# A chunked retention layer with an expert layer behind it: the first 128 tokens of each sequence as one piece, a shorter warm-up, and another list of loads

## The chip, the cores and the metric

The kernel runs on one core of a Trainium2 chip. The metric is the device time of one execution in microseconds (us). The core has five engines that run their own instruction queues side by side: PE (TensorE, matrix products, with the weight loads shown apart as PEld), DVE (VectorE), ACT (ScalarE), POOL (GpSimd) and SP (SyncE, which here only issues DMAs). They meet through semaphores. Results of PE land in PSUM, everything else lies in SBUF, and DMAs bring data in from HBM.

## The reference

Two layers. The first is retention with a decay per head, here 4 sequences, 8 heads, 768 tokens, 64 numbers a head; the second a gated two-matrix layer on the 3072 tokens, 512 to 2048 to 512.

```python
for t in range(S):
    state = gamma[None, :, None, None] * state + np.einsum('bhd,bhe->bhde', k[:, :, t], v[:, :, t])
    y[:, :, t] = scale * np.einsum('bhd,bhde->bhe', q[:, :, t], state)
...
h = x @ w_in
relu6 = np.clip(h + 3.0, 0.0, 6.0)
g = h * relu6 / 6.0
return (g @ w_out).astype(np.float32)
```

## The kernel before

**Rows.** A row is 128 tokens of one sequence with all 8 heads; there are 24. Rows 0 to 3 are the first rows of the four sequences, rows 4 to 7 the second ones, and so on; four rows are one unit u of 512 tokens. A row has four loads of 256 KB: q and k with the head's numbers on the partitions (qt, kt), k and v with tokens on the partitions (kn, vn). A row is cut into two halves of 64 tokens. On PE, `scores` (L374) makes k times q for each half, `gather` (L398) k times v, which is what the row adds to the state, and `inner_part` (L386) applies the masked scores to v; each is 16 small products, and a float32 product is two instructions with a weight load each, so that a block shows as 32. `outer_part` (L361) adds what the earlier state gives; a sequence's first row has none. The decay is put on v before its use (`decay` in `load`: ACT L468, POOL L465) and taken off the result after it (`scale` in `inner_step`, L627, with the table dq). Between them DVE masks the scores (`fading`, L536), ACT passes the part that needs no mask (L541) and copies a first state (L572). The scaled result is then split for the next layer into a high part on ACT (L255) and a low part on DVE (L165); the split pair is x.

**The layers behind.** `mm1_step` (L648) makes one block of 128 of the 2048 columns for a unit: 12 products of 128 x 512 (L656), followed by L662 and L665 and a store to HBM. It needs all four x of its unit and its own block of w_in. These blocks come as 64-bit numbers of 512 KB, and `convert` (L191) with `split` makes a pair of float32 parts of them: ACT L204, DVE L208, L212, L223, L229, ACT L255, DVE L165. The staging tile st has two buffers, so that the load of block 2 waits until block 0 has passed L229, and block 3 waits for block 1. When all 1152 products of the first layer are done, 1008 of the second (L842) follow.

**Order.** Every step is an entry with an engine, a cost, what it needs and a rank. `Plan.order` (L71) runs them through a list schedule ahead of the build, and each engine's queue is then in that order by hand. PE keeps the order in which its steps were added (in `burst`, L687): scores of a row ahead of the inner part of the row before it; then the blocks of unit 0 with rows 4 to 7 between them, and then blocks of units 0 and 1 in turn. SP issues in the order of the list FIRST (L416): v, k, q, k by token of each row in turn, with the table dq and blocks 1 to 4 of w_in behind rows 1, 3, 4, 5 and 7 (BEHIND). An issue that waits holds all behind it. Where the plan sees PE idle in the first 60 us, `spin` (L755) puts products of zeros there; WARM products of zeros stand ahead of everything (L341).

Of the kernel before, what the change touches and what calls it, by code (L numbers as in the profile page):

```python
# [41 lines left out]
class Plan:  # L42
# [28 lines left out]
    def order(self):  # L71
# [43 lines left out]
def retention_ffn(ctx: ExitStack, tc: tile.TileContext, qkv, w_in, w_out, dvs, dqs, out, B, H, S, D):  # L115
# [133 lines left out]

    def split_step(parts, cols, dep, rank, boxes):  # L250


        def high():
            for hi, lo, src in parts():
                nc.scalar.activation(out=hi, in_=src, func=AF.Copy)  # L255
# [7 lines left out]
        return add("DVE", cost - 0.02, low, (one,), rank, boxes, port=True)  # L263

# [8 lines left out]
    def place_box(tag):  # L273

        return plan.box(tag, PLACES[tag])
# [65 lines left out]
    for n in range(WARM):  # L341
        nc.tensor.matmul(idle[:, 0:P], warm[:, 0], warm[:, 1], start=True, stop=True)
# [4 lines left out]
    rows, early, early_boxes, tiles_done = {}, {}, {}, []  # L347

# [25 lines left out]
    def scores(t, wide):  # L374

        for i, c, a, h in tiles:
            nc.tensor.matmul(  # L377
                t["sc"](a, i, c)[halves[h ^ a]],
                t["kt"]["t"][halves[h], 2 * i + a, cut[c]],
                t["qt"]["t"][halves[h], 2 * i + a, whole_or_cut(c, wide)],  # L380
                start=True,
                stop=True,
                skip_group_check=True,
            )

    def inner_part(t, n, wide):  # L386

        for i, c, a, h in tiles:
            nc.tensor.matmul(  # L389
                t["y"][halves[a], h, i, whole_or_cut(c, wide)],  # L390
                t["vn"]["t"][halves[h ^ a], 2 * i + a, cut[c]],
                t["masked"](a, i, c)[halves[h ^ a]],
                start=wide and not n and (i, c) == (0, 0),
                stop=True,
                skip_group_check=True,
            )

    def gather(t, n, wide):  # L398

        for i, c, a, h in tiles:  # L400
            if not c or n < ROWS_B - 1:
# [13 lines left out]

    FIRST = [(0, "vn"), ("w", 0), (0, "kt"), (0, "qt"), (0, "kn")]  # L416
    for r in range(1, AHEAD):
        FIRST += [(r, "vn"), (r, "kt"), (r, "qt"), (r, "kn")]
        FIRST += BEHIND.get(r, [])

# [26 lines left out]
    def load(r, rank):  # L447
# [3 lines left out]
        row = r % UR * ROWS_B + n  # L451
        if r % UR == 0:
            dq[n] = load_part("dq", dqs[n], (0, 17, 34)[n] if n < 3 else None, first(n, "dq", rank - 2))
        t["dq"] = dq[n]
        places = [o for o in range(35) if o not in (0, 17, 34)]
        parts = {"kt": 1, "qt": 0, "vn": 3, "kn": 2}
        for i, (x, which) in enumerate(parts.items()):
            o = places[4 * r + i] if r < AHEAD else None
            t[x], t["box", x], t["got", x] = load_part(x, qkv[row, which], o, first(r, x, rank + i / 10))

        def decay(pool, hs):
            v = t["vn"]["t"].rearrange("p a (h e) -> p (a h) e", h=2)[:, hs]
            scale = cst_sb[:, n, hs]
            if pool:
                nc.gpsimd.tensor_tensor(out=v, in0=v, in1=scale[:, :, None].to_broadcast([P, hs.stop - hs.start, D]), op=ALU.mult)  # L465
            else:
# [7 lines left out]
                lambda *_, pool=pool, hs=hs: decay(pool, hs),  # L474
                (t["got", "vn"],),
                rank + FADE,
                (t["box", "vn"],),
            )
# [3 lines left out]
    def scores_step(r, at):  # L482
# [5 lines left out]
        def run():  # L488
            if spare:
                banks = [ps_h.tile([P, UT], F32, tag="h", name=nm("sc")) for _ in range(2)]  # L490
            else:
                both = ps_a.tile([P, 2, UT], F32, tag="sc", name=nm("sc"))
                banks = [both[:, a] for a in range(2)]
            t["banks"] = [(both, slice(0, 2))] if not spare else [(b[:, None], slice(a, a + 1)) for a, b in enumerate(banks)]
            if wide:
# [6 lines left out]

        t["S"] = add("PE", 0.7 if wide else 0.5, run, (t["got", "kt"], t["got", "qt"]), at, (*t["sc box"], t["box", "kt"], t["box", "qt"]))

# [87 lines left out]
    def outer_step(r, at):  # L592
# [11 lines left out]
        states = ([] if wide else [t["state box", 0]]) + ([was["state box", 1]] if n else [])  # L604
        deps = [None if wide else t["adds"][0], t["S"], was and was["adds"][1]]
        t["T"] = add("PE", 0.55, run, deps, at, (t["y box"], t["box", "qt"], *states))

    def inner_step(r, at):
        t, u, wide = rows[r], r // UR, r < AHEAD
        n = u  # L610

        def run():
# [5 lines left out]

        t["I"] = add("PE", 0.7 if wide else 0.55, run, (*t["A"], t["T"]), at, (t["y box"], t["am box"], t["box", "vn"]))
        if r % UR == 0:  # L620
            x_boxes[u] = [place_box("wf") for a in range(2)] if u == 2 else [plan.box("x", 2)]
            x_ready[u] = []
        xr = plan.box("xr", 2)
# [10 lines left out]
        def parts():  # L634
            if u not in xs and u == 2:
                xs[u] = [place([P, NK, UT], F32R, nm("x"), "wf") for a in range(2)]
            elif u not in xs:
                x = xpool.tile([P, 2, NK, UT], F32R, tag="x", name=nm("x"))
                xs[u] = [x[:, a] for a in range(2)]
            o = r % UR * P  # L640
            yield *(xs[u][a][:, :, o : o + P] for a in range(2)), t["x"]

# [286 lines left out]
def constants(H, S, D):  # L929

    g = 1.0 - 2.0 ** (-5.0 - np.arange(H, dtype=np.float64))
    t = np.arange(S, dtype=np.float64).reshape(S // P, P) - S // 2
    dv = by_half((g[:, None] ** -t.reshape(-1))[:, :, None]).transpose(1, 0, 2).reshape(P, -1)
    dq = (g[:, None] ** t[:, None, :] / np.sqrt(D))[:, heads(H)]
    dq = np.repeat(dq, D, axis=2).transpose(0, 2, 1, 3).reshape(S // P, 2 * D, -1)
    half = P // 2
    mask = np.tile(np.arange(half)[:, None] <= np.arange(half), (2, 1)).astype(np.float64)
# [18 lines left out]
def lay_qkv(q, k, v):  # L956
# [5 lines left out]

    k_half, v_half = (by_half(a).reshape(-1, P, H * D) for a in (k, v))
    return np.ascontiguousarray(np.stack([by_dim(q), by_dim(k), k_half, v_half], axis=1))
# [38 lines left out]
```

## Time and profile before

| what | us |
|---|---|
| median of three runs | 583.24 |
| lowest and highest of them | 581.8, 583.39 |
| the profiled execution, its own time | 584.08 |
| span of the profile of that execution | 582.3 |
| products of the first layer, L656, busy | 268.0 |
| products of the second layer, L842, busy | 233.2 |

The profile's page lists busy time by engine, the span in 40 slices, the chain that ended last and the costliest groups. The windows view gives each engine's busy time in chosen stretches, the mean clock granted to TensorE (1.00 is full) and the share of the DMA engines that was in use. The timeline lists instructions in order; behind each group, in brackets, stand the idle time of its engine just before it and what ended that. "issue" there means that the engine waited for nothing that the profile shows. A "q" behind an engine's name marks its queue, where DMAs are issued.

### The profile page before, as it was taken

What the parts mean: (1) busy time and instruction counts of PE and PEld (TensorE: products, weight loads), DVE (VectorE), ACT (ScalarE), POOL (GpSimd) and SP (SyncE); (2) the same over time, 40 slices, a digit from 0 to 9 for tenths busy, and PEclk for the clock granted to TensorE, in tenths of its full rate; (3) what the DMA queues carried; (4) which work ended last, traced back from release to release, by engine and by line L of the source; (5) the groups of instructions that cost most, each with busy time, mean ns of one, the idle gap of its engine ahead of it and who ended that gap; (6) DMA issues with size and microseconds to landing.
All of it is one profiled execution on the core that took longest, in us unless ns stands there. A gap on an engine that the chain in (4) does not pass through costs nothing.

```text
span 582.3 us, 12762 instructions
## 1 busy us (share of the span) xinstructions
PE 567.6 (97%) x5102; PEld 467.0 (80%) x5102; DVE 420.3 (72%) x752; ACT 245.3 (42%) x442; POOL 19.7 (3%) x25
## 2 busy tenths in 40 slices
PE   7699999999999999999999999999999999999997
PEld 6577888888888888888888888888888888888885
DVE  4389988989843798443445967997699966799753
ACT  5484454544422443222244544454434443454340
POOL 1000000001000000001000000000000000000000
PEclk9699999999999999999999999999999999999999
DMA  9685587676744576554255439974789546897002
GB/s 324 260 298 193 180 282 262 190 274 228 236 146 163 197 225 221 175 178 168 75 181 181 163 118 350 373 226 130 255 260 314 178 110 196 281 312 223 1 4 105
DMA packets 61259, 119.91 MB, mean 206 GB/s; under 512 B 7056, under 2 KB 7312, under 8 KB 61200
## 3 DMA queue, kind: packets, MB, share of 16 engines
q1 hardware_dynamic: 60912, 119.04, 60.6%
q8 instruction: 40, 0.66, 0.5%
q14 instruction: 19, 0.16, 0.1%
q10 hardware_dynamic: 288, 0.06, 0.0%
HBM read 87.61 MB, written 31.46 MB: 204 GB/s over the span
## 4 chain that ended last, share of the span: by engine, by line
PE 95%; DMA 2%; issue 1%; DVE 1%; SPq 0%; DVEq 0%
PE h L656 46%; PE o L842 40%; PE y L389 3%; PE sc L377 3%; PE sc L402 2%; DMA early<-in_qkv 2%; PE y L365 2%; PE spin L758 0%; SPq L189 0%; DVE wb L223 0%; PE pace L355 0%; DVE ww L229 0%; DVE xr L627 0%; DVE x L165 0%; DVE u L859 0%
## 5 line engine op out<-in xcount | busy, mean ns | idle before, releaser
L656 PE MATMUL h<-x,w 128*128 128x512 f32 x1152 | 268.0, 392 | 0.6 <-DVE x L165 0.6
L656 PEld LDWEIGHTS h<-x,w 128*128 128x128 f32 x1152 | 214.6, 188 | 46.2 <-DVE x L165 1.0
L842 PE MATMUL o<-gc,w 128*128 128x512 f32 x1008 | 233.2, 393 | 0.0
L842 PEld LDWEIGHTS o<-gc,w 128*128 128x128 f32 x1008 | 189.2, 188 | 43.8
L665 DVE SCALAR_TENSOR_TENSOR g<-g,h 128x512 f32<-128x512 f32 x96 | 65.8, 686 | 80.3 <-ACT g L662 79.5
L662 ACT ACTIVATE g<-h,three 128x512 f32<-128x512 f32 x96 | 66.0, 688 | 117.0 <-PE h L656 116.7
L247 ACT ACTIVATE gc<-gr 128x512 fp32r<-128x512 f32 x120 | 71.6, 623 | 58.4 <-PE o L842 42.2
L165 DVE TENSOR_TENSOR gc<-gr,gc 128x512 fp32r<-128x512 f32 x120 | 79.6, 685 | 21.2 <-ACT gc L247 21.0
L247 ACT ACTIVATE gc<-keep 128x512 fp32r<-128x512 f32 x48 | 30.3, 632 | 63.7 <-PE o L842 41.3
L165 DVE TENSOR_TENSOR gc<-keep,gc 128x512 fp32r<-128x512 f32 x48 | 32.8, 686 | 12.4 <-ACT gc L247 12.2
L204 ACT ACTIVATE wm<-st 128x512 f32<-128x512 f32 x32 | 21.5, 671 | 20.3 <-DMA st<-in_w_out 8.7
L255 ACT ACTIVATE x<-xr 128x512 fp32r<-128x512 f32 x24 | 15.1, 629 | 31.6 <-DVE xr L627 31.6
L465 POOL TENSOR_TENSOR vn<-vn,cst_sb 128x512 f32<-128x512 f32 x16 | 16.9, 1058 | 244.4 <-DMA vn<-in_qkv 219.5
L859 DVE SCALAR_TENSOR_TENSOR u<-o,u 128x512 f32<-128x512 f32 (+1 forms) x31 | 20.1, 666 | 6.4 <-PE o L842 6.4
L223 DVE SCALAR_TENSOR_TENSOR wb<-st,wb 128x512 int32<-128x512 int32 x32 | 22.7, 710 | 0.4
L165 DVE TENSOR_TENSOR w<-ww,w 128x384 fp32r<-128x384 f32 (+2 forms) x34 | 22.1, 656 | 0.8 <-ACT w L255 0.7
L229 DVE SCALAR_TENSOR_TENSOR ww<-st,wb 128x512 int32<-128x512 int32 x32 | 21.9, 685 | 0.3
L168 DVE TENSOR_TENSOR keep<-gr,gr 128x512 f32<-128x512 f32 x24 | 16.4, 685 | 7.0 <-DMA gr<-gd 7.0
L255 ACT ACTIVATE w<-ww 128x384 fp32r<-128x384 f32 (+2 forms) x34 | 18.5, 550 | 6.2 <-DVE ww L229 6.0
L208 DVE TENSOR_SCALAR wm<-wm 128x512 f32<-128x512 f32 x32 | 14.1, 441 | 8.6 <-ACT wm L204 8.3
L165 DVE TENSOR_TENSOR x<-xr,x 128x512 fp32r<-128x512 f32 x24 | 16.5, 688 | 2.6 <-ACT x L255 1.8
L536 DVE TENSOR_TENSOR am<-sc,mask 128x512 f32<-128x512 f32 (+1 forms) x26 | 16.5, 640 | 2.1 <-PE sc L402 1.7
(52 smaller groups left out, 334.4 us busy)
## 6 DMA issues: line engine op xcount, KB each, us to landing
gr<-gd SPq DMA_DIRECT2D x168, 256.0 KB, 4.3
gd<-g SPq DMA_DIRECT2D x96, 256.0 KB, 2.8
early<-in_qkv SPq DMA_DIRECT2D x32, 256.0 KB, 5.6
st<-in_w_in SPq DMA_DIRECT2D x16, 512.0 KB, 4.1
st<-in_w_out SPq DMA_DIRECT2D x16, 512.0 KB, 3.9
kt<-in_qkv SPq DMA_DIRECT2D x16, 256.0 KB, 3.4
qt<-in_qkv SPq DMA_DIRECT2D x16, 256.0 KB, 4.5
vn<-in_qkv SPq DMA_DIRECT2D x16, 256.0 KB, 5.3
```

The lines of the kernel that those rows point to most:

```text
L165: return nc.vector.tensor_tensor(out=out_, in0=a, in1=b, op=ALU.subtract)
L204: nc.scalar.activation(out=t["m"], in_=t["hi"].bitcast(F32), func=AF.Abs)
L223: nc.vector.scalar_tensor_tensor(out=b, in0=t["hi"], scalar=-0x40000000, in1=b, op0=ALU.bitwise_and, op1=ALU.bitwise_or)
L229: nc.vector.scalar_tensor_tensor(out=t["w"].bitcast(I32), in0=t["lo"], scalar=29, in1=t["b"], op0=ALU.logical_shift_right, op1=ALU.bitwise_or,
L247: nc.scalar.activation(out=hi, in_=src, func=AF.Copy)
L255: nc.scalar.activation(out=hi, in_=src, func=AF.Copy)
L377: nc.tensor.matmul(t["sc"](a, i, c)[halves[h ^ a]], t["kt"]["t"][halves[h], 2 * i + a, cut[c]], t["qt"]["t"][halves[h], 2 * i + a, whole_o ...
L656: nc.tensor.matmul(h, w[:, o, a], xs[u][b][:, k], start=k + n == 0, stop=(k, n) == (NK - 1, 2), skip_group_check=True)
L662: nc.scalar.activation(out=t["g"], in_=t["h"], func=AF.Relu, bias=three)
L665: ins = nc.vector.scalar_tensor_tensor(out=t["g"], in0=t["g"], scalar=6.0, in1=t["h"], op0=ALU.min, op1=ALU.mult)
L842: nc.tensor.matmul(banks[b, i, h], w2c[jj][:, RIGHT[i], a, h], gc[:, q, c], start=jj == 0 and n == 0, stop=jj == NFP - 1 and n == 2, skip_ ...
L859: nc.vector.scalar_tensor_tensor(out=out_[:, cut], in0=banks[b, i, h][:, cut], scalar=f, in1=other[:, cut], op0=ALU.mult, op1=ALU.add)
```

## The change

For rows 0 to 3 (n = 0, "whole") the row is no longer halved. Scores are 8 products with the full 128 tokens on both sides, the inner part is 8, the gather is 8. The table m0, m1 (two loads of 256 KB instead of the one table dq of that unit) holds the decay between each pair of tokens by head together with the mask and the scale, and DVE multiplies the scores by it in two instructions of 512 columns. So neither v's decay nor the scaling afterwards is needed: x is split straight out of PSUM. For the state, k by token is given its decay (same instructions as v had), and the gather of row r moves from the row's own turn to the turn of row r + 4 (`states_step`); its result is copied by ACT into the space of the row's kt. Masked scores have three buffers in a place of w_in blocks, and all of rows 0 to 3 share one PSUM tile for their results. The host lays k, v and the tables out accordingly.

The warm-up has 4 products of 512 columns instead of 14 of 128. The list of the first loads is written out: k, q, m0, m1, v, w_in block 0, and so on (t is k by token, d is dq, w a block). The plan lets SP start at 0.7 instead of 2.0 us, and three of its ranks are new.

```diff
-        free = dict.fromkeys(left, self.FIRST)
+        free = {e: 0.7 if e == "SP" else self.FIRST for e in left}
...
-    WARM = 14
+    WARM = 4
     SPIN, FILL = 60.0, 0.7
     DECAY = ("ap", "ap", "ap", "ap", "aa", "aa", "aa", "aa")
-    FADE, W_FIRST, W_NEXT = 4.5, 0.5, 2.0
-    BEHIND = {1: [(0, "dq")], 3: [("w", 1)], 4: [(1, "dq"), ("w", 2)], 5: [("w", 3)], 7: [("w", 4)]}
+    FADE, W_FIRST, W_NEXT = 2.5, 1.5, 1.0
+    KFADE = 7.0
+    ORDER = "k0 q0 m0 m1 v0 w0 k1 q1 v1 k2 q2 v2 t0 k3 q3 v3 w1 t1 v4 t2 t3 k4 q4 t4 d1 v5 k5 q5 t5 w2 w3 k6 q6 t6 v7 k7 v6 q7 t7 w4"
...
-        nc.tensor.matmul(idle[:, 0:P], warm[:, 0], warm[:, 1], start=True, stop=True)
+        nc.tensor.matmul(idle, warm[:, 0], warm, start=True, stop=True)
...
+        if t["whole"]:
+            for p in range(NPAIR):
+                for h, d in enumerate(halves):
+                    nc.tensor.matmul(
+                        t["banks"][h][:, p * P : (p + 1) * P],
+                        t["kt"]["t"][d, p],
+                        t["qt"]["t"][d, p],
+                        start=True,
+                        stop=True,
+                        skip_group_check=True,
+                    )
+            return
...
+            for h, d in enumerate(halves):
+                for p in range(NPAIR):
+                    i, a = divmod(p, 2)
+                    nc.tensor.matmul(
+                        t["ys"][halves[a], (2 * h + i) * P : (2 * h + i + 1) * P],
+                        t["vn"]["t"][:, p, d],
+                        t["am"][:, h, p],
+                        start=True,
+                        stop=True,
+                        skip_group_check=True,
+                    )
...
+            for p in range(NPAIR):
+                i, a = divmod(p, 2)
+                for d in halves:
+                    nc.tensor.matmul(
+                        t["us"][d, a, i],
+                        t["kn"]["t"][:, p, d],
+                        t["vn"]["t"][:, p, d],
+                        start=True,
+                        stop=True,
+                        skip_group_check=True,
+                    )
+            return
...
-        if r % UR == 0:
-            dq[n] = load_part("dq", dqs[n], (0, 17, 34)[n] if n < 3 else None, first(n, "dq", rank - 2))
-        t["dq"] = dq[n]
+        if r == 0:
+            dq[0] = [load_part("dq", dqs[h * ROWS_B], 34 * h, first("m", h, 0)) for h in range(2)]
+        elif r % UR == 0:
+            dq[n] = load_part("dq", dqs[n], 17 if n == 1 else None, first(n, "dq", rank - 2))
+        t["dq"], t["whole"] = dq[n], not n
...
+        what = "vn" if n else "kn"
+
         def decay(pool, hs):
-            v = t["vn"]["t"].rearrange("p a (h e) -> p (a h) e", h=2)[:, hs]
+            v = t[what]["t"].rearrange("p a (h e) -> p (a h) e", h=2)[:, hs]
...
-                rank + FADE,
-                (t["box", "vn"],),
+                (t["got", what],),
+                rank + (FADE if n else KFADE),
+                (t["box", what],),
...
+    def masks_step(r, at):
+        t = rows[r]
+        t["am box"] = plan.box("ams", NAM)
+
+        def fading():
+            if not ams:
+                big = place([P, NAM, 2, NPAIR, P], F32, nm("ams"), "w")
+                ams.extend(big[:, n] for n in range(NAM))
+            t["am"] = ams[r % NAM]
+            for h in range(2):
+                nc.vector.tensor_tensor(
+                    out=t["am"][:, h].rearrange("p a n -> p (a n)"),
+                    in0=t["banks"][h],
+                    in1=t["dq"][h][0]["t"].rearrange("p a n -> p (a n)"),
+                    op=ALU.mult,
+                )
+
+        deps, boxes = [t["S"], *(m[2] for m in t["dq"])], [*t["sc box"], t["am box"], ams_box, *(m[1] for m in t["dq"])]
+        t["A"] = [add("DVE", 1.22, fading, deps, at + 2, boxes)]
+
+    def states_step(r, at):
+        t, box = rows[r], plan.box("h", NH)
+        t["state box", 1] = t["box", "kt"]
+
+        def run():
+            us = ps_h.tile([P, UT], F32, tag="h", name=nm("us"))
+            t["us"] = us[:, 0 : 2 * P].rearrange("p (a i n) -> p a i n", a=2, i=2)
+            gather(t, 0, True)
+
+        def copy():
+            t["state", 1] = t["kt"]["t"][:, 0:2].rearrange("p i (a n) -> p i a n", a=2)
+            nc.scalar.activation(out=t["state", 1], in_=t["us"], func=AF.Copy)
+
+        t["G"] = add("PE", 0.6, run, (*t["faded"], t["got", "kn"], t["got", "vn"]), at, (box, t["box", "kn"], t["box", "vn"]))
+        t["adds"] = {1: add("ACT", 0.37, copy, (t["G"],), at + 1.5, (box, t["state box", 1]))}
...
+            t["y box"] = plan.box("y0", 2)
+
+            def run():
+                if not whole_ys:
+                    whole_ys.append(ps_a.tile([P, 2, UT], F32, tag="y", name=nm("y")))
+                t["ys"] = whole_ys[0][:, r % 2]
+                inner_part(t, n, wide)
+
+            def parts():
+                yield *x_parts(u, r * P), t["ys"].rearrange("p (a n) -> p a n", n=P)
+
+            t["I"] = add("PE", 1.1, run, (*t["A"], t["got", "vn"]), at, (t["y box"], t["am box"], ams_box, t["box", "vn"]))
+            x_ready[u].append(split_step(parts, [4 * P], t["I"], at + 1, (t["y box"], *x_boxes[u]), port=False))
...
+            if UR <= new < AHEAD:
+                states_step(new - UR, n - 0.1)
             scores_step(new, n)
-        if old is not None:
+        if old is not None and not rows[old]["whole"]:
             outer_step(old, n + 0.1)
         if new is not None:
-            gather_step(new, n + 0.2)
+            (masks_step if rows[new]["whole"] else gather_step)(new, n + 0.2)
```

More of the change, by code (lines that the diff above doesn't have):

```diff
@@ L262, in split_step @@
         one = add("ACT", cost, high, (dep,), rank, boxes)
-        return add("DVE", cost - 0.02, low, (one,), rank, boxes, port=True)
+        return add("DVE", cost - 0.02, low, (one,), rank, boxes, port=port)
     w1s, w1_boxes, w1_ready = {}, {}, {}
@@ L341, in retention_ffn @@
     for n in range(WARM):
-        nc.tensor.matmul(idle[:, 0:P], warm[:, 0], warm[:, 1], start=True, stop=True)
+        nc.tensor.matmul(idle, warm[:, 0], warm, start=True, stop=True)
     halves = [slice(h * D, (h + 1) * D) for h in range(2)]
     mask = apool.tile([P, HALF], F32, name="mask", bufs=1)
-    rows, early, early_boxes, tiles_done = {}, {}, {}, []
+    rows, early, early_boxes, tiles_done, ams, whole_ys = {}, {}, {}, [], [], []
+    NAM, ams_box = 3, place_box("w")
     tiles = [(i, c, a, h) for i in range(2) for c in range(2) for a in (1, 0) for h in range(2)]
@@ L386, in inner_part @@
     def inner_part(t, n, wide):
+        if t["whole"]:
+            for h, d in enumerate(halves):
[10 more added lines that the diff above has]
+            return
         for i, c, a, h in tiles:
@@ L398, in gather @@
     def gather(t, n, wide):
+        if t["whole"]:
+            for p in range(NPAIR):
[9 more added lines that the diff above has]
+                    )
+            return
         for i, c, a, h in tiles:
@@ L414, in early_tile @@
         return early[key]
[L416 to L419, printed above, removed]
+    LOADS = {"q": "qt", "k": "kt", "t": "kn", "v": "vn", "d": "dq"}
+    FIRST = [(x[0], int(x[1])) if x[0] in "mw" else (int(x[1]), LOADS[x[0]]) for x in ORDER.split()]
     def first(r, x, rank):
@@ L493, in run @@
                 banks = [both[:, a] for a in range(2)]
+            if t["whole"]:
+                t["banks"] = banks
+                return scores(t, wide)
             t["banks"] = [(both, slice(0, 2))] if not spare else [(b[:, None], slice(a, a + 1)) for a, b in enumerate(banks)]
@@ L501, in run @@
             scores(t, wide)
-        t["S"] = add("PE", 0.7 if wide else 0.5, run, (t["got", "kt"], t["got", "qt"]), at, (*t["sc box"], t["box", "kt"], t["box", "qt"]))
+        t["S"] = add("PE", 1.1 if t["whole"] else 0.7 if wide else 0.5, run, (t["got", "kt"], t["got", "qt"]), at, (*t["sc box"], t["box", "kt"], t["box", "qt"]))
+    def masks_step(r, at):
[27 more added lines that the diff above has]
+        t["adds"] = {1: add("ACT", 0.37, copy, (t["G"],), at + 1.5, (box, t["state box", 1]))}
     def gather_step(r, at):
@@ L604, in outer_step, with x_parts @@
         states = ([] if wide else [t["state box", 0]]) + ([was["state box", 1]] if n else [])
-        deps = [None if wide else t["adds"][0], t["S"], was and was["adds"][1]]
+        deps = [None if wide else t["adds"][0], t["S"], was and was["adds"][1], *(x_ready[0] if r == UR else [])]
         t["T"] = add("PE", 0.55, run, deps, at, (t["y box"], t["box", "qt"], *states))
+    def x_parts(u, o):
+        if u not in xs and u == 2:
+            xs[u] = [place([P, NK, UT], F32R, nm("x"), "wf") for a in range(2)]
+        elif u not in xs:
+            x = xpool.tile([P, 2, NK, UT], F32R, tag="x", name=nm("x"))
+            xs[u] = [x[:, a] for a in range(2)]
+        return (xs[u][a][:, :, o : o + P] for a in range(2))
     def inner_step(r, at):
@@ L610, in inner_step @@
         n = u
+        if r % UR == 0:
+            x_boxes[u] = [place_box("wf") for a in range(2)] if u == 2 else [plan.box("x", 2)]
+            x_ready[u] = []
+        if t["whole"]:
+            t["y box"] = plan.box("y0", 2)
[8 more added lines that the diff above has]
+            x_ready[u].append(split_step(parts, [4 * P], t["I"], at + 1, (t["y box"], *x_boxes[u]), port=False))
+            return
         def run():
@@ L617, in run @@
             inner_part(t, n, wide)
[L619 to L622, printed above, removed]
+        deps = x_ready[0] if r == UR else []
+        t["I"] = add("PE", 0.7 if wide else 0.55, run, (*t["A"], t["T"], *deps), at, (t["y box"], t["am box"], t["box", "vn"]))
         xr = plan.box("xr", 2)
@@ L634, in parts @@
         def parts():
[L635 to L641, printed above, removed]
+            yield *x_parts(u, r % UR * P), t["x"]
         one = add("DVE", 0.61, scale, (t["I"], t["dq"][2]), at + 1, (t["y box"], t["dq"][1], xr))
@@ L932, in constants @@
     t = np.arange(S, dtype=np.float64).reshape(S // P, P) - S // 2
-    dv = by_half((g[:, None] ** -t.reshape(-1))[:, :, None]).transpose(1, 0, 2).reshape(P, -1)
+    dv = by_half((g[:, None] ** -t.reshape(-1))[:, :, None])
+    dv[0] = (g[:, None] ** -t[0]).T
+    dv = dv.transpose(1, 0, 2).reshape(P, -1)
     dq = (g[:, None] ** t[:, None, :] / np.sqrt(D))[:, heads(H)]
     dq = np.repeat(dq, D, axis=2).transpose(0, 2, 1, 3).reshape(S // P, 2 * D, -1)
+    gap = np.arange(P) - np.arange(P)[:, None]
+    whole = np.where(gap >= 0, g[:, None, None] ** np.maximum(gap, 0), 0.0) / np.sqrt(D)
+    whole = whole.reshape(-1, 2, P, P).transpose(1, 2, 0, 3).reshape(2, P, -1)
+    dq = np.concatenate([whole[:1], dq.reshape(S // P, P, -1)[1:], whole[1:]])
     half = P // 2
@@ L961, in by_dim, with by_token @@
         return a.reshape(B, H // 2, 2, S // P, P, D).transpose(0, 3, 2, 5, 1, 4).reshape(-1, 2 * D, H // 2 * P)
-    k_half, v_half = (by_half(a).reshape(-1, P, H * D) for a in (k, v))
+    def by_token(a):
+        n = by_half(a)
+        n[:, 0] = a[:, :, :P].transpose(0, 2, 1, 3).reshape(B, P, -1)
+        return n.reshape(-1, P, H * D)
+    k_half, v_half = by_token(k), by_token(v)
     return np.ascontiguousarray(np.stack([by_dim(q), by_dim(k), k_half, v_half], axis=1))
```

3 lines of the change are left out of this document (1 added, 2 removed).

## The prediction

> **What bounds the kernel now.** I read the page first, then the windows view (columns: window, length, busy time and products of PE and PEld, busy time of DVE, ACT and POOL, granted clock, DMA share, GB/s).
>
> ```profile
> span 582.3 us, 12762 instructions
> 31.22:55.73 24.51, 23.43 (x513) 19.37 (x513) 20.79 (x40) 16.34 (x45) 1.04 (x1) 1.00 0.75 270
> 62.57:296.40 233.83, 233.77 (x2849) 194.09 (x2849) 158.60 (x302) 87.28 (x138) 15.88 (x15) 1.00 0.59 199
> ```
>
> From 62.57 to 296.40 PE is idle for 0.06 us, and the second layer follows as densely. No work there is touched, so it can only be shifted. What the change is worth lies ahead: by how much does PE reach the same point in its queue earlier? I take as that point the end of rows 4 to 7 between the first four blocks, where the dense blocks begin: 55.73. Call the start of the first full block T (31.22 now) and that point D. Then the timeline for the stretch ahead of T:
>
> ```profile
> 1.45 4.75 PE L342 MATMUL idle<-warm 128*128 128x128 f32 x28 [1.45 <-DVE warm L339]
> 7.63 0.90 PE L377 MATMUL sc<-early 64*64 64x128 f32 x32 [1.42 <-DMA early<-in_qkv]
> 16.85 0.33 PE L377 MATMUL sc<-early 64*64 64x64 f32 x3 [2.27 <-issue]
> 18.26 1.57 PE L377 MATMUL sc<-early,early 64*64 64x128 f32 x32
> 23.31 0.38 PE L402 MATMUL sc<-early 64*64 64x64 f32 x3 [2.72 <-issue]
> 27.01 1.46 PE L389 MATMUL y<-am,early 64*64 64x128 f32 x32
> 31.22 2.77 PE L656 MATMUL h<-x,w 128*128 128x512 f32 x11 [0.59 <-DVE x L165]
> ```
>
> Two holes of 2.27 and 2.72 us with no releaser cut through row 2's scores and row 3's gather, in the middle of one step. The windows up to the first hole and between the two, and the DMA view in three quarter-microseconds (14.00, 20.75 and 24.25), say what they are:
>
> ```profile
> 0.00:14.60 14.60, 10.29 (x221) 9.12 (x221) 6.06 (x11) 7.82 (x23) 2.14 (x8) 1.00 0.92 324
> 16.80:20.60 3.80, 3.74 (x126) 3.56 (x126) 1.29 (x2) 1.02 (x3) 0.00 (x0) 0.66 1.06 396
> 20.60:23.30 2.70, 0.00 (x0) 0.00 (x0) 0.69 (x1) 0.26 (x1) 0.00 (x0) 0.50 1.03 385
> q8 instruction: 40, 0.66, 0.5%
> q8 instruction: 1, 0.02, 27.0%
> q8 instruction: 1, 0.02, 27.7%
> q8 instruction: 1, 0.02, 32.1%
> ```
>
> Between the holes PE ran 126 products and 126 weight loads, 252 instructions. The instruction queue moves 0.66 MB / 40 = 16.5 KB a packet. A packet runs at 14.0 and at 20.75, and PE goes on 2.6 to 2.9 us later, at 16.85 and 23.31. I read it so: PE's program comes in pages of some 252 instructions; a page is asked for when the last but one is used up (16.85 for the packet at 20.75), and while the DMA engines are full (share 1.03 to 1.06) it takes 23.31 - 16.85 = 6.46 us. With empty queues the packet of 24.25 follows its request at 23.31 by 0.9 us. Rows 0 to 3 eat a page in 3.8 us, so PE starves. The first hole comes after 442 instructions, 252 + 190.
>
> The second delay is on SP: the page's waits for the DMA queue, the timeline of POOL (whose row shows when a row's v has landed), DVE and SP, and one window.
>
> ```profile
> 8.91 0.61 POOL L465 TENSOR_TENSOR early<-early,cst_sb 128x256 f32<-128x256 f32 x1 [4.49 <-DMA early<-in_qkv]
> 14.96 0.61 POOL L465 TENSOR_TENSOR early<-early,cst_sb 128x256 f32<-128x256 f32 x1 [2.09 <-DMA early<-in_qkv]
> 26.43 0.41 DVE L208 TENSOR_SCALAR wm<-wm 128x512 f32<-128x512 f32 x1
> 29.87 0.69 DVE L229 SCALAR_TENSOR_TENSOR ww<-st,wb 128x512 int32<-128x512 int32 x1
> SPq L189 <- DVE ww L229: 13.0, 2, 9.9
> 30.62 0.33 SPq L189 DMA_DIRECT2D st<-in_w_in  x1
> 25.00:30.60 5.60, 5.60 (x47) 4.12 (x45) 4.65 (x10) 4.20 (x14) 0.00 (x0) 0.71 0.02 7
> ```
>
> Block 1's conversion sits in DVE's queue behind row 3's mask, which waits for the second hole; L229 ends at 30.56, SP waits 9.9 us for it with block 3's load, and the DMA engines stand empty (0.02).
>
> **The change, step by step.** *Landing.* In units of 256 KB (a block of w_in is 2), v of row 1 was unit 7 and seen at 8.91, v of row 3 unit 16 at 14.96: 0.672 us a unit. In the new list v0 is unit 5, q1 9, q3 16, v3 17, w1 19, t4 26, t5 31, w2 33, w3 35, v6 41, t7 43, w4 45. By that line q1 is there at 10.25, q3 at 14.96, v3 at 15.6, w1 at 17.0, t4 at 21.7, t5 at 25.0, w2 at 26.4, w3 at 27.7, v6 at 31.8, w4 at 34.4. The first ones land sooner, but the warm-up covers them: it streams 4 x 2 x 512 = 4096 columns where 28 x 128 = 3584 took 4.75, so 5.4, and ends at 6.9, ahead of the 7.63 of now. Nothing is lost there.
>
> *Instructions.* Until row 3's inner part the queue now has 16 for the warm-up and 4 x 64 (two blocks of 8 products a row, each two instructions and two loads) = 272, and some 20 of zero products. The first 190 last until about 13.5, within row 1's inner part; the page then asked for is there at 13.5 + 6.5 = 20, and is wanted only after 252 more: row 2 and 3 (106), a block (24), row 0's gather (32), row 4's scores (64), in all until about 24. **Both holes go**, 5.0 us; late next is the landing of q3.
>
> *The chain of row 3.*
>
> ```profile
> L536 DVE TENSOR_TENSOR am<-sc,mask 128x512 f32<-128x512 f32 x2 | 1.4, 686 | 1.7 <-PE sc L402 1.7
> L627 DVE TENSOR_TENSOR xr<-y,early 128x512 f32<-128x512 f32 x4 | 2.8, 692 | 9.1 <-PE y L389 9.1
> L165 DVE TENSOR_TENSOR x<-xr,x 128x512 fp32r<-128x512 f32 x4 | 2.8, 688 | 1.0 <-ACT x L255 1.0
> L255 ACT ACTIVATE x<-xr 128x512 fp32r<-128x512 f32 x4 | 2.5, 623 | 1.1 <-DVE xr L627 1.1
> L468 ACT ACTIVATE early<-early,cst_sb 128x64 f32<-128x64 f32 x32 | 8.3, 334 | 5.0 <-DMA early<-in_qkv 4.0 <-DMA cst_sb<-in_decays_v 1.0
> L204 ACT ACTIVATE wm<-st 128x512 f32<-128x512 f32 x3 | 2.0, 668 | 0.2 <-DMA st<-in_w_in 0.2
> 8.31 0.68 PE L402 MATMUL sc<-early 64*64 64x64 f32 x32
> ```
>
> The new products (64 x 128 and 128 x 64 weights) are in no row. Two of them fit side by side in the array, four of the old ones did, so 16 instructions should cost what 32 did: 0.90. The other end is no pairing at all, 4.75 / 28 = 0.17 each, 2.7 a block. I take 0.95, next to the row with the same amount of arithmetic. Then: scores 14.96 to 15.9; two masks at 0.69, 17.35; inner part, 18.3; ACT 0.62 straight from PSUM, 19.0; DVE 0.69, 19.8; hops of up to 0.1 at each step (L229's end at 30.56 to SP's issue took 0.06) and up to one foreign instruction of 0.69 on DVE ahead: **T = 20.5**. DVE per row loses the mask (0.69) and the scaling (0.69) and gets two masks, so nothing; from 7 to 20 it has 4 x 2.07 and block 0's 2.9, 11.2 of 13 us. ACT loses the passing of scores; its decays (4 x 0.334 a row, POOL beside it) move behind t, off row 3's chain. The second mask table is one unit more, in the list above.
>
> *From T to D.* The same blocks and rows took 24.51 with PE busy for 23.43. Four gathers move in, 32 instructions took 0.68 from start to end, 16 wide ones 0.5: 2.0, so 26.5 without a new wait. Is there one? Block 1 lands at 17.0, its conversion (two of 0.41 and three of 0.69 on DVE, 2.9; 0.67 and 0.62 on ACT) ends near 22, ahead of its use at 25.5, so SP reaches block 3 at about 21 with no wait to speak of. Block 2 (26.4 + some 5 for ACT, DVE, ACT, DVE) is ready at 31.5, wanted at 32. Row 6 wants v6, 31.8 plus 8 x 0.334 on ACT = 34.5, at 35. Each is just in time. DVE has 20.79 and the rest of block 1, some 22 of 28 us. The narrowest is PE's own program: 2 x 513 + 4 x 32 = 1154 instructions, 4.6 pages, at 6.46 each 29.6 us if the DMA engines stay full; they do until w4 at 34.4, half of the stretch. Already now a page is just in time here, with a row that I would expect to see grow:
>
> ```profile
> 40.51 0.90 PE L389 MATMUL y<-am,early 64*64 64x128 f32 x32 [0.38 <-issue]
> ```
>
> Between 26.5 and 29.6 I take 28.5: **D = 49.0**, that is 55.73 - 49.0 = 6.7 us earlier. The rest (a table of the third unit that goes to another buffer, the new ranks, SP's start in the plan) is in the order alone; below and above it may be a late or lucky place in a queue, within the bounds of T and D.
>
> **The sum.** The profiled execution took 584.08, 0.84 above the median of 583.24. 584.08 - 6.7 = 577.4, and against the median **576.5**.
>
> **The rivals.**
> *It runs clean* (574.0): no page is late, T = 20.0, D = 46.5, 9.2 us. For it: every landing above is ahead of its use. Against it: the 0.38 that is there today.
> *Half clock* (579.8). The clock fell to 0.66 and 0.50 around the holes, and scores took 1.57 and the inner part 1.46 instead of 0.90. If PE, with its waits for landings between 7 and 20, falls back too, row 3 pays 0.6 + 0.6 and the first block 0.7 x 3.0 (2.77 for 11 of its 12 products) = 2.1: D = 52.3. Against it:
>
> ```profile
> 7.50:16.00 8.50, 5.54 (x193) 4.55 (x193) 4.03 (x7) 5.57 (x20) 1.84 (x3) 1.00 1.05 394
> ```
>
> PE was busy for only 65% here and kept 1.00; it will have about 7.6 of 13 us and zero products besides. Products that do not pair end in the same place.
> *The holes stay* (581.5): if they are not the program's pages, 5.0 us come back, D = 54.0, 1.7 us earlier. [...]
> *Slower: block 1's conversion ends as late as now* (585.2). Place: DVE's queue, and SP's behind it. If L229 of block 1 again comes after something late, block 3 and the eight loads of rows 6 and 7 behind it wait as now, D stays at 55.73 and the four gathers come on top: 2.0 us later. It begins to cost when that L229 ends after 22, has taken the whole gain at 28.7, and is slower by more than 0.3% from 30.5 on. For it: it was 9.9 us. Against it: what it stood behind, row 3's mask, was late through the hole.
>
> **How the numbers follow.** Forecast 0.57, clean 0.17, half clock or unpaired 0.15, holes stay 0.06, slower 0.05. The range reaches from the clean case to just past half clock, 573.5 to 580.5, and leaves out the last two and the edges. About 0.3%, 1.75 us, is what can be told from no change. Faster by more than that: the first three and a sixth of the fourth, 0.90; within it 0.05; slower 0.05.
>
> **What would show it.** T near 20.5 and no "issue" idle above 1 us ahead of it; packets of the instruction queue near 17 and 28; block 3's issue on SP before 23 and DMA share near 1 up to 34; D near 49 and 233.8 us for the dense stretch as now. An L229 wait on SP of several us, a clock under 0.9 between 10 and 25, or blocks that wait for w_in would prove a step wrong.

## The result

| | us |
|---|---|
| before, median (lowest, highest) | 583.23 (581.8, 583.39) |
| changed, median (lowest, highest) | 577.72 (576.79, 577.86) |
| ratio, 95% interval | 0.9908 (0.9889 to 0.9926) |
| changed, profiled execution, its own time | 576.79 |

5.5 us faster by the medians, 0.9%; forecast were 6.7 us and 576.5. Between the two profiled executions it is 7.3 us, 584.08 to 576.79; why these differ from the medians is answered below by the eleventh run.

The page's first line and three rows of the windows view of the changed kernel (columns as in the prediction):

```profile
span 575.0 us, 12332 instructions
```

```profile
0.00:14.60 14.60, 12.22 (x88) 8.01 (x90) 6.19 (x11) 3.79 (x7) 0.91 (x6) 1.00 0.88 313
21.90:48.34 26.44, 26.12 (x579) 21.89 (x579) 21.05 (x39) 20.96 (x62) 1.04 (x1) 1.00 0.84 300
55.05:289.00 233.95, 233.89 (x2858) 194.16 (x2849) 159.56 (x304) 87.28 (x139) 16.06 (x15) 1.00 0.60 200
```

The dense stretch is what it was, 233.9 us with 0.06 us idle. PE made 88 products until 14.60 where it had made 221, with the clock at 1.00. Rows of the timeline of PE, from row 0's scores to the first of the dense blocks (others left out):

```profile
6.55 1.16 PE L381 MATMUL sc<-early 64*128 64x128 f32 x16
15.30 1.16 PE L381 MATMUL sc<-early,early 64*128 64x128 f32 x16
18.59 1.09 PE L406 MATMUL y<-ams,early 128*64 128x128 f32 x16 [0.70 <-ACT x L256]
21.17 0.50 PE L756 MATMUL h<-x,w 128*128 128x512 f32 x1 [0.43 <-ACT x L256]
21.90 2.79 PE L756 MATMUL h<-x,w 128*128 128x512 f32 x11 [0.23 <-DVE x L166]
24.62 0.69 PE L431 MATMUL us<-early 128*64 128x64 f32 x16
25.24 0.90 PE L391 MATMUL sc<-early 64*64 64x128 f32 x32
48.34 5.73 PE L756 MATMUL h<-x,w 128*128 128x512 f32 x24
```

T, the first full block, moved from 31.22 to 21.90, and D, the start of the dense blocks, from 55.73 to 48.34. No "issue" row stands ahead of T. From T to D it takes 26.44 instead of 24.51, since the four gathers lie there now. SP did not wait for block 1 for long:

```profile
21.81 1.02 SPq L190 DMA_DIRECT2D st<-in_w_in  x2
```

Both loads, blocks 2 and 3, go out by 22.8, where block 3's went out at 30.62.

**One number for a run.** In all fourteen profiles of this study (two of the kernel before, two of the changed one, ten others) the run's own time less D is 528.35 to 528.52: 584.08 - 55.73 = 528.35, 576.79 - 48.34 = 528.45. So D decides, and below each run is told by its T and D.

### The profile page after: what moved, and what is told of

The parts are those of the page before. It is cut to its first block, busy times and chain, and to the rows that moved or that the text cites. A ratio compares the mean times of both kernels' runs of the same rounds, so it can differ in the third digit from the quotient of the medians.

```text
span 575.0 us, 12332 instructions
## 1 busy us (share of the span) xinstructions
PE 566.8 (99%) x4890; PEld 463.3 (81%) x4890; DVE 420.1 (73%) x750; ACT 243.1 (42%) x434; POOL 20.1 (4%) x25
## 4 chain that ended last, share of the span: by engine, by line
PE 96%; DMA 2%; DVE 1%; ACT 0%; issue 0%; DVEq 0%; SPq 0%
PE h L756 46%; PE o L944 41%; PE sc L391 2%; PE y L416 2%; PE sc L442 2%; PE y L367 2%; DMA early<-in_qkv 1%; DMA cst_sb<-in_decays_v 1%; DVE x L166 0%; DVE ams L560 0%; PE us L431 0%; PE y L406 0%; ACT x L256 0%; PE sc L381 0%; DVE xr L733 0%
## 5 line engine op out<-in xcount | busy, mean ns | idle before, releaser
L256 ACT ACTIVATE x<-xr 128x512 fp32r<-128x512 f32 x20 | 12.6, 630 | 26.8 <-DVE xr L733 26.8
L224 DVE SCALAR_TENSOR_TENSOR wb<-st,wb 128x512 int32<-128x512 int32 x32 | 22.8, 712 | 0.3
L230 DVE SCALAR_TENSOR_TENSOR ww<-st,wb 128x512 int32<-128x512 int32 x32 | 22.3, 698 | 0.3
L169 DVE TENSOR_TENSOR keep<-gr,gr 128x512 f32<-128x512 f32 x24 | 16.3, 684 | 5.4 <-DMA gr<-gd 5.4
L166 DVE TENSOR_TENSOR keep<-keep,gr 128x512 f32<-128x512 f32 x24 | 16.3, 682 | 0.8 <-DMA gr<-gd 0.7
L166 DVE TENSOR_TENSOR gr<-gr,gr 128x512 f32<-128x512 f32 x24 | 16.4, 682 | 0.1
```

The lines of the kernel that those rows point to most:

```text
L166: return nc.vector.tensor_tensor(out=out_, in0=a, in1=b, op=ALU.subtract)
L224: nc.vector.scalar_tensor_tensor(out=b, in0=t["hi"], scalar=-0x40000000, in1=b, op0=ALU.bitwise_and, op1=ALU.bitwise_or)
L230: nc.vector.scalar_tensor_tensor(out=t["w"].bitcast(I32), in0=t["lo"], scalar=29, in1=t["b"], op0=ALU.logical_shift_right, op1=ALU.bitwise_or,
```

## The experiments

Theory: PE's program comes in pages of 126 products with their weight loads; the second page ends with product 221, and while the DMA engines are full, rows 0 to 3 of the kernel before use a page faster than the next arrives. Rivals: the holes belong to the old steps or their data; or the gain is that of the list of loads and the ranks.

**1. The warm-up alone, in the kernel before.**

```diff
-    WARM = 14
+    WARM = 4
-        nc.tensor.matmul(idle[:, 0:P], warm[:, 0], warm[:, 1], start=True, stop=True)
+        nc.tensor.matmul(idle, warm[:, 0], warm, start=True, stop=True)
```

> The kernel before with the changed warm-up alone: 4 zero products of 512 columns in place of 14 of 128, which is 40 instructions fewer on PE and nothing else. If the two holes are pages of PE's program, they keep their distance from the start in instructions and so move 40 instructions (20 products with their weight loads) further: the first from product 29 of row 2's scores to about product 17 of row 2's gather, the second from product 27 of row 3's gather to about product 15 of row 2's inner part. If they belong to the steps or to their data, they stay at the same products. Both: time within 1 us of before.

583.68 us (one run), beside a median of 581.87 for before on that chip (580.69 to 584.16 in 13 runs): within its range, but not within the 1 us that was expected. The timeline of PE at the two holes:

```profile
13.90 0.45 PE L402 MATMUL sc<-early 64*64 64x64 f32 x16
16.62 0.40 PE L402 MATMUL sc<-early 64*64 64x64 f32 x13 [2.27 <-issue]
...
19.18 0.56 PE L389 MATMUL y<-am,early 64*64 64x128 f32 x15 [0.29 <-DVE am L536]
22.56 1.01 PE L389 MATMUL y<-am,early 64*64 64x64 f32 x17 [2.82 <-issue]
```

The holes moved by 20 products, from 29 of row 2's scores to 16 of its gather (all of the scores are ahead of it), and from 27 of row 3's gather to 15 of row 2's inner part. Neither step, data nor engine changed there, only what lies ahead in the queue. By count the first is again behind the product 220 or 221 (8 + 32 + 32 + 2 + 32 + 32 + 32 + 2 + 32 + 16 = 220; some records are missing in traces). The steps as a cause fall.

**2. Everything but the whole rows.**

```diff
-        free = dict.fromkeys(left, self.FIRST)
+        free = {e: 0.7 if e == "SP" else self.FIRST for e in left}
...
-    WARM = 14
+    WARM = 4
...
-    FADE, W_FIRST, W_NEXT = 4.5, 0.5, 2.0
+    FADE, W_FIRST, W_NEXT = 2.5, 1.5, 1.0
...
+    ORDER = "k0 q0 v0 t0 w0 k1 q1 v1 t1 d0 k2 q2 v2 t2 k3 q3 v3 t3 w1 v4 k4 q4 t4 d1 v5 k5 q5 t5 w2 w3 k6 q6 t6 v7 k7 v6 q7 t7 w4"
```

The warm-up's product is edited as in the first run, and the list of loads is read from ORDER.

> The kernel before with everything of the change but the whole rows: the warm-up, the ranks, SP's start in the plan and the new list of loads (k by token straight behind v, since a row's mask waits for its gather here). If the gain comes from fewer instructions, the holes are still there (5 us in all), the first full block still starts near 31 and the time is at most 1.5 us below before. If the list and the ranks are what gains, block 1's conversion ends before 24, and some 5 us are gained.

581.86 us, ratio to before 1.000 (0.9983 to 1.0017): the list, the ranks and the warm-up together give nothing that shows without the whole rows. In the profiled execution (581.07, near the lowest of ten, 581.01 to 584.1) T is 27.96 and D 52.65:

```profile
19.24 0.48 PE L389 MATMUL y<-am,early 64*64 64x128 f32 x9 [0.21 <-ACT am L539]
21.39 0.68 PE L389 MATMUL y<-am,early 64*64 64x64 f32 x23 [1.66 <-issue]
...
52.65 5.78 PE L654 MATMUL h<-x,w 128*128 128x512 f32 x24
```

The second hole is there, 126 products behind the 221st, at the ninth of row 2's inner part. The first is gone though the rows have as many instructions as before: row 2's gather waits 0.57 us for a decay, and PE comes to product 221 at 15.78, some 2.5 us behind the packet of 13.25, just as the next page does. So the expected "5 us in all" was wrong for this order, where 1.66 are left; that no gain results held.

**3. The changed kernel with the old order of loads.**

```diff
-    ORDER = "k0 q0 m0 m1 v0 w0 k1 q1 v1 k2 q2 v2 t0 k3 q3 v3 w1 t1 v4 t2 t3 ...
+    ORDER = "v0 w0 k0 q0 m0 m1 t0 v1 k1 q1 t1 v2 k2 q2 t2 v3 k3 q3 t3 w1 v4 ...
```

> The changed kernel with the loads in the old order (v, block 0, k, q, then the two mask tables, k by token; then row by row). If fewer instructions are what gains, no hole comes back, and the first full block starts later only by the landing of row 3's q, three units of 256 KB or 2.0 us: from 21.9 to 23.9, the dense blocks from 48.3 to about 50.3, time 2 us above the changed kernel and still 3.5 below before. If the list is what gains, the start goes back to about 30 and the time to that of before.

577.91 us, ratio 0.9919 (0.9894 to 0.9943), as good as the changed kernel within the intervals. No hole ahead of T, T at 22.76 instead of the 23.9 that were expected, D at 49.48:

```profile
16.40 1.16 PE L381 MATMUL sc<-early,early 64*128 64x128 f32 x16 [0.53 <-DMA early<-in_qkv]
22.76 2.83 PE L756 MATMUL h<-x,w 128*128 128x512 f32 x11 [0.22 <-DVE x L166]
...
33.16 0.34 PE L442 MATMUL sc<-early 64*64 64x64 f32 x6 [0.37 <-issue]
...
49.48 5.78 PE L756 MATMUL h<-x,w 128*128 128x512 f32 x24
```

Row 3's scores begin 1.1 us later, not 2.0. With the second run: the whole rows carry the gain, the list 0.6 to 1.1 us of D (48.34 and 48.86 in the two profiles of the changed kernel).

The row at 33.16 is a late page in a kernel with whole rows: an idle time with no releaser behind product 344, where a page's end is due (221 and 126 are 347), 2.4 us behind a packet of the instruction queue that ran at 30.75.

**4 and 8. A PSUM tile for each row's result.** In the changed kernel rows 0 to 3 share one tile of two halves.

```diff
-        ys = ps_a.tile([P, 2, UT], F32, tag="y", name=nm("y"))[:, :, 0 : 2 * P]
-        t["ys"], t["y"] = ys, ys.rearrange("p h (i n) -> p h i n", i=2)
+        t["ys"] = [ps_a.tile([P, UT], F32, tag="y", name=nm("y"), bufs=2)[:, 0 : 2 * P] for h in range(2)]
+        t["y"] = [ys.rearrange("p (i n) -> p i n", i=2) for ys in t["ys"]]
...
-                if not whole_ys:
-                    whole_ys.append(ps_a.tile([P, 2, UT], F32, tag="y", name=nm("y")))
-                t["ys"] = whole_ys[0][:, r % 2]
+                t["ys"] = ps_a.tile([P, UT], F32, tag="y", name=nm("y"), bufs=2)
```

The later rows get two such tiles as well, and their scaling is two instructions of 256 columns instead of one of 512. That part lies behind T.

> The changed kernel with a PSUM tile of its own for each row's result instead of two halves of one tile (later rows use two such tiles, and their scaling is two instructions of 256 columns). If rows 2 and 3 wait for each other's split only because they share the tile, row 3's inner part starts with its mask (18.0 instead of 18.6), row 2's low part no longer waits for it, and the first block starts at about 20.9 instead of 21.9; the time falls by 1.0 us. If these waits come from the order of semaphore counts on DVE and ACT, nothing moves.

575.88 us, ratio 0.9885 (0.9862 to 0.9908). D is 47.40. The waits of PE in the changed kernel, then the timeline of the second execution of this version:

```profile
PE y L406 <- DVE x L166: 0.8, 2, 0.4
PE y L406 <- ACT x L256: 0.7, 1, 0.7
```

```profile
17.31 1.26 PE L406 MATMUL y<-ams,early 128*64 128x128 f32 x16 [0.17 <-DVE ams L560]
21.33 2.79 PE L755 MATMUL h<-x,w 128*128 128x512 f32 x11 [0.23 <-DVE x L166]
47.78 4.42 PE L755 MATMUL h<-x,w 128*128 128x512 f32 x18
```

In the changed kernel the inner part of rows 1 to 3 waits for the split of the row before it (x, on DVE or ACT), which uses the other half: 0.8 us in two waits and 0.7 in one. With tiles of their own only the row's mask (ams) is waited for. To compare on one chip, both ran again:

> The changed kernel again, beside the two that follow, on one chip. If its time is what lies ahead of the dense blocks plus a fixed 528.4 us, its span's dense stretch starts at 48.3 to 49.4 again.

> The changed kernel with a PSUM tile of its own for each row's result, again. If the shared tile costs 1 us of the start, it is 1.0 us (0.17%) below the changed kernel on the same chip.

577.31 us for the changed kernel (ratio 0.9912, 0.9893 to 0.9931), 576.28 for this version (0.9891, 0.9876 to 0.9906): 1.0 us. The intervals of the ratios overlap, but T is 22.35 against 21.33 and 21.90 against 20.96, and D 48.86 against 47.78 and 48.34 against 47.40. This is the best version of the study, beside the next, which is no different.

**9. Row 0's k by token later**, in the version of run 8.

```diff
-... k2 q2 v2 t0 k3 q3 v3 w1 t1 ...
+... k2 q2 v2 k3 q3 v3 t0 w1 t1 ...
```

> As the run before, with row 0's k by token loaded behind row 3's v instead of ahead of row 3's k. If the landing of row 3's q sets the start, it lands one unit, 0.67 us, earlier and the dense blocks start 0.5 us earlier. If DVE, which has no idle time from 12 to 22 there, sets it, nothing moves.

576.46 us (0.9889, 0.9872 to 0.9906): nothing. T is 21.23, against 21.33, and row 3's scores begin at 14.81 instead of 14.95, not 0.67 earlier. So the landing of row 3's q does not set T any more. DVE's queue, busy for 9.59 of the 10.00 us from 12 to 22 in run 8, would fit; it was not tried. In the profiled execution, the slowest of the five (577.52), D is 49.06, behind run 8's 47.78, since PE waits for row 7's scaling there:

```profile
47.11 0.90 PE L367 MATMUL y<-early,early 64*64 64x128 f32 x16 [1.46 <-DVE xr L732]
```

**5 and 6. More instructions on PE.** The plan's zero products are left out in both, and behind the scores of rows 0 to 2 stand other ones.

```diff
-    SPIN, FILL = 60.0, 0.7
+    SPIN, FILL = 0.0, 0.7
...
+        for n in range(24):
+            nc.tensor.matmul(t[halves[n % 2], 0:32], warm[:, 0, 0:D], warm[:, 1, 0:32], start=True, stop=True)
```

The sixth run has three `nc.tensor.matmul(t[:, 0 : 2 * P], warm[:, 0], warm[:, 1:3], ...)` in that place.

> The changed kernel, with the plan's zero products left out and, behind the scores of rows 0, 1 and 2, 24 zero products of 32 columns each: 48 products and 48 weight loads on PE a time, 288 instructions in all, no data and no other engine touched. If PE's program in pages makes the holes, row 0 to 3 is again longer than the two pages that PE holds at the start: the second page is used up at about 15, the third is there at about 18, and an idle time of 2 to 3.5 us with no releaser stands ahead of or in row 1's inner part or row 3's scores; the first full block starts 2 us or more later than in the run with few instructions of the same length. If the number of instructions is of no account, the two runs start within 0.5 us of each other.

> The counterpart of the run before: at the same three places 3 zero products of 256 columns, 12 instructions a time, about as long on PE (1.3 us). Under both theories no hole; the first full block starts at 22 to 23 (21.9 in the changed kernel).

580.68 and 579.95 us (one run each). The expected hole of 2 to 3.5 us did not come. The timeline of the run with many, and its DMA view at 13.75:

```profile
14.49 1.59 PE L528 MATMUL pad<-warm 128*64 128x32 f32 x48
15.92 1.34 PE L406 MATMUL y<-ams,early 128*64 128x128 f32 x16
```

```profile
q8 instruction: 1, 0.02, 27.4%
```

The packet of the third page ran at 13.75, and pages were usable some 2.6 us behind their packet in run 1 (14.00 to 16.62), so here at 16.35. PE came to product 221, the fifth of this inner part, at about 16.3: products 220 and 221 start 0.22 us apart, where the pairs around them follow in 0.10, and the part took 1.34 instead of the 1.07 to 1.09 of the others. A page ends where it should, but PE hardly outran the fetch here, with 5.2 us from product 95 to product 221, and the first product of the first block starts at 23.05 against 23.41. My arithmetic had that page 1.7 us later than it came. Number of instructions alone is not the cost. What stands ahead of a hole is 126 products and their loads used up sooner than the next page is there: in the seven holes ahead of T in the two profiles of before and in runs 1 and 2, PE went on 5.6 to 6.8 us behind the product that stands 126 ahead of the hole.

Both runs are slower than the changed kernel, by 2.2 and 3.0 us, with D at 52.28 and 51.54. The first block starts at 23.05 and 23.41, later than the 21.17 of the changed kernel and than the 22 to 23 expected of the sixth run, since row 3's scores stand behind the padding (17.19 and 17.54 instead of 15.30). The rest is the clock. Without the plan's zero products (1.13 us of them stand ahead of the first block in the changed kernel) PE idles there for 1.49 us, and the granted clock falls. Windows of the run with many:

```profile
18.00:23.00 5.00, 2.54 (x40) 1.86 (x36) 4.23 (x7) 2.82 (x8) 1.93 (x3) 0.97 1.07 377
23.00:29.00 6.00, 5.95 (x16) 4.03 (x18) 1.98 (x3) 4.45 (x18) 0.00 (x0) 0.50 0.88 320
```

The first block ran at a clock of 0.50 and took 5.79 us instead of 3.0; in the run with few the clock was 0.70 from 23.4 to 29.0. So the rival "half clock" can come true here. That the zero products keep it away is a guess of mine and not shown: both runs have the padding too, and no run leaves out the zero products alone.

**10. The same arithmetic in twice the products.**

```diff
-                        t["qt"]["t"][d, p],
+                        t["qt"]["t"][d, p, cut[c]],
...
-                        t["am"][:, h, p],
+                                t["am"][:, h, 2 * i + a, cut[c]],
```

> The changed kernel with each score and inner product of rows 0 to 3 made as two of 64 columns: the same data, steps and arithmetic, 32 instead of 16 products a block. If a page of PE's program ends with product 221 and the next is there 5.3 to 6.5 us after product 95, an idle time of 0.3 to 1.6 us with no releaser comes back, at product 11 of row 2's inner part and nowhere else ahead of the first full block, which starts up to 1.5 us later than the 21.9 to 22.4 of the changed kernel. If the holes came from the old steps (gather in between, scaling), none appears.

579.95 us, ratio 0.9958 (0.9944 to 0.9972), T 25.04, D 51.51, and no hole: a miss for the theory's numbers, for a reason that the timeline shows.

```profile
14.87 2.00 PE L382 MATMUL sc<-early 64*128 64x64 f32 x32
16.80 1.15 PE L409 MATMUL y<-ams,early 128*64 128x64 f32 x32
```

Scores in two halves take 2.00 instead of 1.16, the inner part 1.15 and 1.09. From the start of the scores to the start of the next step a product takes 60 ns (16.80 - 14.87 over 32), where it took 69 with 128 streamed columns (1.10 over 16); an inner product takes 34 instead of 64. So half the columns are half the time for the inner part, but hardly less for the scores, whose weights are 128 columns wide instead of 64. A load of these weights takes 188 ns, one of the inner part's 137 (medians of L381 and L406 in the changed kernel); whether that is the cause was not tried apart. The scores took nearly twice as long, and PE came to product 221 only at about 20, after a packet that ran at 16.50. The test could not tell the theories apart.

**11. The kernel before, profiled again.**

> The kernel before, profiled once more. If a run's time is the start of the dense blocks plus 528.4 us and the scatter of its runs comes from the length of the two holes, the holes are again at product 221 and 126 products later, and the start of the dense blocks differs from 55.73 by as much as the time differs from 584.08.

```profile
16.45 0.33 PE L377 MATMUL sc<-early 64*64 64x64 f32 x3 [2.54 <-issue]
22.40 0.28 PE L402 MATMUL sc<-early 64*64 64x64 f32 x3 [1.76 <-issue]
39.18 0.90 PE L389 MATMUL y<-am,early 64*64 64x128 f32 x32 [0.95 <-issue]
45.43 0.22 PE L355 MATMUL pace<-mask 64*64 64x4 f32 x1 [0.52 <-issue]
54.66 5.51 PE L656 MATMUL h<-x,w 128*128 128x512 f32 x23
```

583.01 us. The holes are at the same products, and 2.54 and 1.76 us long (2.27 and 2.72 before). D is 54.66: 1.07 less than in the profile that the prediction used, and the time is 1.07 less. The profile that the prediction used was one of the longer runs, and D of the median of 583.24 lies near 583.24 - 528.4 = 54.8. The two holes together are 0.7 us shorter here, and T is 29.28, 1.9 earlier. Of that 0.9 is lost again from T to D, nearly all of it in the two waits with no releaser behind products 600 and 727, 0.95 and 0.52 here and 0.38 and 0.31 (at 40.51 and 46.51) in the other profile. They are the ends of later pages: 221 and three and four times 126 are 599 and 725. What else moved T was not traced.

**12. The old ranks in the changed kernel.**

```diff
-    FADE, W_FIRST, W_NEXT = 2.5, 1.5, 1.0
+    FADE, W_FIRST, W_NEXT = 4.5, 0.5, 2.0
-        free = {e: 0.7 if e == "SP" else self.FIRST for e in left}
+        free = dict.fromkeys(left, self.FIRST)
```

> The changed kernel with the three ranks and SP's start in the plan of the kernel before. If these only order what is ready at once, block 1's conversion still ends near 22 and the time is within 0.7 us of the changed kernel. If they keep block 1's conversion ahead, L230 of block 1 ends some us later, SP's issue of block 3 with it, and the dense blocks start 1 us or more later.

579.07 us, ratio 0.9943 (0.9925 to 0.9961), against 0.9908 and 0.9912 of the changed kernel. T is 22.14, as with the new ranks; the windows from T to D, and PE's waits:

```profile
22.14:50.62 28.48, 27.21 (x584) 22.52 (x584) 22.26 (x42) 21.52 (x63) 1.04 (x1) 1.00 0.80 286
```

```profile
PE y L367 <- ACT w L256: 1.2, 1, 1.2
```

Neither expectation fits. Block 1's L230 ends at 22.7, so nothing is lost there; but the stretch behind T takes 28.48 instead of 26.44. ACT makes the high part of block 2 behind a decay of a later row, at 32.30 instead of 31.06, and PE stands behind ACT once more at the end of row 7. So the ranks and SP's start in the plan are worth some 2 us of D with the whole rows, on ACT. What they are worth without them was not tried alone.

## Why the prediction held, and where it did not

- **The bound and the shift.** Right: the dense part is unchanged, and the time is D plus 528.4 in every profile.
- **Both holes go.** Right, and for the reason given: they are ends of pages, at product 221 and 126 products on, and they move with the count (runs 1 and 2) and stay with it (run 11). No run made them come back ahead of T in the changed kernel; runs 5 and 10 were meant to and could not, and a hole of 0.37 us further on in run 3 is the nearest to it. In the changed kernel the third page's packet ran at 18.25, so it was usable at about 20.9, and product 221 was reached at about 26, in row 4's gather. PE stood after 442 instructions by count (not in run 2) and 252 further on, for 1.66 to 2.82 us at a time. No trace records when a page is asked for; "when the last but one is used up" was my estimate from the packets, which ran 3.7 and 3.9 us behind the starts of products 96 and 222 in the first profile of before (10.3 to 14.00, 16.85 to 20.75), and about 3.1 behind products 96 and 222 in the changed kernel (15.1 to 18.25, 26.15 to 29.25). The 0.9 us that I gave for empty queues came from queues that were still emptying (DMA share 0.79 from 23.50, 0.41 from 24.00); no sum uses it.
- **The chain of row 3 and T.** 20.5 forecast, 21.9 measured. The scores began at 15.30 instead of 14.96. The step "inner part, 18.3" failed, it ended at 19.7: PE did not start with the mask's end (17.94) but at 18.59, behind row 2's split, and row 2's low part waited for that inner part in turn, 0.75 us on DVE. I had read the box of two halves in the plan as two buffers; they are two halves of one tile, and runs 4 and 8 show that it costs 1.0 us. The scores at 1.16 and the inner part at 1.09 instead of 0.95 are 0.35 more. What "side by side" is worth was measured in the rate alone: 0.95 ns a streamed column in ten zero products at 128*128 (2.43 us from 7.65 on), 0.57 in a block of scores at 64*128 (1.16), 0.29 in one of before at 64*64 (0.90).
- **From T to D.** 28.5 forecast, 26.44 measured: the 2.0 for late pages was the mis-sized term: no wait for a page shows in the timeline any more. The 26.5 without a wait came out partly by luck: a gather took 0.62 instead of 0.5 (24.62 to 25.24), 2.5 in all, while the two late pages of before, 0.38 and 0.31, went. I had charged a full fetch for each of 4.6 pages, though PE had a page in hand at T (the packet of 18.25) and a block of 24 instructions takes 3 us. But it was close: the packet of 29.25 was in just in time for the product behind the 344th, which starts at 31.82, 0.15 us after the one ahead of it, and in run 3 the same page was 0.37 us late.
- **The sum.** The two errors, 1.4 too early and 2.1 too long, are of opposite sign, and by that luck D is near: 49.0 forecast, 48.34 and 48.86 measured. What put the median 1.2 us above the forecast is the last term, which took the gain from a profile with D = 55.73 and set it against a median whose D is 54.8. By the second pair of profiles (54.66 and 48.86) the gain is 5.8 us, and 5.5 was measured.
- **The ranks, "in the order alone".** Right in kind, but not small: run 12 puts them at about 2 us of D. The sum was not hurt, since it took for granted that each load and decay is "just in time", and with the new ranks they are.
- **Rivals.** Half clock did not come (1.00 in every window shown of the changed kernel); no run shows whether the zero products kept it away (without them, but with the padding, it was 0.50 and 0.70 in runs 5 and 6). L230 of block 1 ended at 22.4. T went 9.3 us ahead, the gathers took 1.9 back, 7.4 remain. How much of the 9.3 is the holes and how much the shorter row (no gather ahead of the mask, no scaling) was not separated by a run. Taking off the holes gives an estimate: 9.3 - 5.0 leaves 4.3 us for the shorter row beside the first profile, 7.4 - 4.3 leaves 3.1 beside run 11, and 6.1 - 1.7 leaves 4.4 beside run 2, which has the new ranks, the new warm-up and nearly the new list. So holes and shorter row would carry about half of the gain in T each, if an idle time ahead of T passes on to T in full.

## What to carry to other kernels

Where many small products run while the DMA engines are full, count instructions between two waits: PE's program came over the same engines here, in packets of 16.5 KB for 126 products with their loads, and a hole with no releaser in the middle of a step (1.66 to 2.82 us here) is read with the instruction queue's packets beside it. Take the median's D, not one profile's, as the base of a sum when the start of a kernel scatters from run to run. Give results that are read at different times tiles of their own, since the halves of one tile waited for each other here, at a cost of 1.0 us (runs 4 and 8).

## What the runs showed of the hardware

- With the DMA engines full (share 1.03 to 1.06 around the holes of before), a page of PE's program came as one packet of 16.5 KB, and PE went on 2.6 to 2.9 us behind its start (14.00 to 16.85 and 20.75 to 23.31 before; 13.75 to 16.45 and 19.75 to 22.40 in run 11).
- A score product here, with weights of 64 x 128, takes 69 ns when 128 columns stream (1.16 us a block of 16) and still 60 when 64 do (2.00 a block of 32); an inner product, with weights of 128 x 64, takes 64 and 34 (1.09 and 1.15).
- The scatter of the kernel before, 580.69 to 584.16 in 13 runs on one chip, lies ahead of its dense part where its two profiles show it (584.08 and 583.01, both 528.35 more than their D); what else than the length of the waits for pages makes it was not tried.
- An idle time of 1.49 us after a thinly used stretch (PE busy 2.54 of 5.00 us) was followed by a clock of 0.50 for about 6 us (run 5); in run 6, with 2.89 of 5.40 busy, the same idle time was followed by 0.70.
